# A fused clustered-attention and two-layer expert kernel: float32 probability tiles, TensorE transposes and a rewritten instruction order

## The chip, the cores and the metric

The kernel runs on one core of one Trainium2 chip. The metric is the device time of one execution in microseconds (us), lower is better.

## The reference, cut to what matters

Three parts follow one another; the output of each is the input of the next.

```
q_assign = argmax(q_n . c_n);  k_assign = argmax(k_n . c_n)      # 16 clusters, per head
scores   = where(q_assign == k_assign, q k^T / 8, -1e9)          # batch 2, 8 heads, 768 x 768, depth 64
x        = softmax(scores) v                                     # -> 1536 tokens x 512
h        = x @ w_in;  g = h * clip(h + 3, 0, 6) / 6              # 512 -> 2048
x        = g @ w_out                                             # 2048 -> 512
logits   = x @ phi                                               # 32 slots (8 experts x 4)
d        = softmax over the tokens;  slot_input = d^T x
slot_out = relu(slot_input @ w1[e]) @ w2[e]                      # 8 experts, 512 -> 1024 -> 512
out      = softmax over the slots(logits) @ slot_out             # 1536 x 512
```

w_in and w_out arrive as float64; w1 and w2 (16.8 MB each) as float32.

## The kernel before, in words

**Order.** The program is a list of some 1,130 generators ("events"), made by `ev(fn, ...)` in the body of the kernel. `ORDER`, a list of event numbers at the top of the file, says which one issues its next step; each engine works through its own instructions in exactly that order, and a semaphore wait holds up all that stands behind it on the same engine or queue. `ROOMS` says which buffer each tile takes. Event numbers, `ORDER` and `ROOMS` were written by a planner and have no loops in them.

**Attention.** There are 16 heads, 8 of batch one (0 to 7) and 8 of batch two. A head's q, k, v are loaded (`load`) and split into a float16 high part (`cast_hi`, ScalarE and VectorE) and a low part (`cast_lo`, L321 on VectorE for batch one, L323 on GpSimd for batch two); a DMA transpose from the SP queue (L361) turns them to `qk1t`. `as_mm` and `as_max` find the clusters, `as_put` (GpSimd, L417, L418) writes them as masks beside the data, and a second DMA transpose (L423) makes `qk2t`. `maxq` multiplies (L460), `maxr` takes each query's maximum on VectorE (L476, 768 columns from PSUM, 96 in all), `shift` (L483, L485) writes it back as six extra rows. `scores` (L498, L502) makes the transposed scores of one of six key tiles, `exps` (L546, L539) their exponential in float32 on ScalarE. A tile then goes one of two ways. Where `WHOLE` holds (batch one, tiles 1 and 4) the float32 tile itself is the stationary operand of six float32 matmuls (L572). Else ScalarE makes a float16 high part (L313), GpSimd a low part (`plow`, L323), and `pv` does 18 float16 matmuls (L577, L578, L585). `cnt_mm` (L432, L434, L435) gives a mean for empty clusters, added by L592 and L593; `finish` divides on VectorE.

**Weights of the first layer.** Each of 8 blocks of w_in and 8 of w_out is narrowed from float64 to float32 by integer operations on VectorE (L799, L802, L807, 1024 columns each), and multiplied on from there (`win`, `wout`, `wphi1` to `wphi3`: w_out is folded with phi to `wp2`).

**Hidden layer and routing.** The tokens are 12 tiles t of 128. Tiles 0 to 5 (batch one) are worked on beside the heads of batch two, tiles 6 to 11 after the last head. `xtrans` turns x by DMA; `hid` does 48 matmuls of 512 columns (L641); `act` applies the nonlinearity (ScalarE L658, VectorE L660, ScalarE L313, GpSimd L323), leaves `ghl` in float16 high and low, and a DMA transpose from the SP queue (L668) turns that to `gt`. `logits` (L678, L679) does 16 pairs of a 64-column and a 32-column matmul; a copy on ScalarE and an addition and a copy on VectorE follow (L682 to L686). `colmax`, `dweights` and `dispatch` (L743) keep a running softmax over the tokens, `cweights` the softmax over the slots.

**Experts and output.** `fetch` (L954, L935) streams w1 and w2 in 512 KB pieces from the SP queue into buffers ("rooms"): 4 of `ring_a`, 11 of `ring_b` that exist once attention's memory is given back (`close`), and 7 that hold the w_in blocks `w0` to `w3`, `ghl` and `gt` until those are no longer read. Pieces wait on the SP queue behind the transposes issued there. `zsum`, `slot_in`, `slot_t`, `layer1` (L1220), `turn`, `layer2` (L1257), `layer2_part` (L1277), `slots_out` and `combine` (L1197, L1205, L1207) finish; `combine_weights` turns its factors with one DMA transpose `cT` on the ScalarE queue (L1151).

Of the kernel before, what the change touches and what calls it, by code (L numbers as in the profile page):

```python
# [199 lines left out]
class Rooms:  # L200
# [6 lines left out]
    def tile(self, shape, dt, **k):  # L207
        room = self.rooms.get(k["name"])
        if room is not None:
            k["tag"] += "." + room  # L210
            k["bufs"] = 1
        return self.pool.tile(shape, dt, **k)


NRA = 4
NRB = 11


# [1132 lines left out]
```

## Time and profile before

| what | before |
|---|---|
| median of 3 runs | 523.71 us (520.7 to 527.46) |
| span of the profiled execution | 523.8 us |
| busy: TensorE (PE) / VectorE (DVE) | 445.6 us / 336.9 us |
| busy: ScalarE (ACT) / GpSimd (POOL) | 296.7 us / 277.5 us |
| moved by DMA | 100.95 MB |
| first hidden matmul / last hidden matmul | 189.6 us / 436.8 us |

The profile is of one execution, whose own time is known by its span alone; the span is within 0.1 us of the median. Busy times are shares in which an engine had an instruction running; matmuls overlap, so the distance from one start to the next says what a matmul costs in a row of them.

### The profile page before, as it was taken

The page shows a single profiled execution, that of the slowest core. Times are in us where ns is not written, and L with a number is a line of the kernel's source. Part 1 is how long each engine was busy: PE and PEld are TensorE (multiplying, and loading weights), DVE is VectorE, ACT ScalarE, POOL GpSimd, SP SyncE. Part 2 cuts the span into 40 slices and gives each one's busy share as a digit, 9 for nine tenths or more (in the row PEclk, how much of TensorE's full clock was granted, in tenths as well). Part 3 has the DMA queues.
Part 4 walks back from the last instruction along what each step waited for, and adds up shares of the span by engine and source line. Part 5 has one row for each costly group of instructions (what it writes and reads, how often), then busy time and mean ns, then how long its engine had stood idle before and what let it go on. Part 6 is the DMA issues. An engine that isn't in the chain of part 4 may idle for free. (4 is left out here: it accounts for less than half of the span.)

```text
span 523.8 us, 11918 instructions
## 1 busy us (share of the span) xinstructions
PE 445.6 (85%) x4892; PEld 268.0 (51%) x4892; DVE 336.9 (64%) x561; ACT 296.7 (57%) x491; POOL 277.5 (53%) x255
## 2 busy tenths in 40 slices
PE   0379898799889888899899999999999995698674
PEld 0225675476666656475665656664444442432152
DVE  4799999969999879997766664545343545401122
ACT  5166677668689788697847578763334445100021
POOL 3212769557799985978757768764235432000000
PEclk9999897769899999999999999999999998688796
DMA  8984564665474699445938632648999999999977
GB/s 215 282 208 87 162 168 124 162 121 147 128 194 143 182 235 228 128 124 120 167 136 146 133 112 48 177 99 159 291 245 258 240 276 265 343 271 369 367 215 230
DMA packets 155638, 100.95 MB, mean 193 GB/s; under 512 B 118208, under 2 KB 141248, under 8 KB 155584
## 3 DMA queue, kind: packets, MB, share of 16 engines
q1 hardware_dynamic: 148896, 93.97, 70.0%
q10 hardware_dynamic: 6688, 6.23, 3.8%
q8 instruction: 38, 0.62, 0.5%
q14 instruction: 16, 0.13, 0.1%
HBM read 64.06 MB, written 7.34 MB: 136 GB/s over the span
## 5 line engine op out<-in xcount | busy, mean ns | idle before, releaser
L323 POOL TENSOR_TENSOR pp<-p,pp 128x768 f16<-128x768 f32 x80 | 145.7, 1828 | 43.8 <-ACT pp L313 28.9
L641 PE MATMUL h<-wq,xt 128*128 128x512 f16 x576 | 134.4, 379 | 0.8 <-DVE r L660 0.5
L476 DVE TENSOR_REDUCE m<-sm 128x1 f32<-128x768 f32 x96 | 89.5, 952 | 27.1 <-PE sm L460 26.6
L546 ACT ACTIVATE p<-st 128x768 f32<-128x768 f32 x80 | 64.6, 810 | 47.8 <-PE st L502 27.8
L641 PEld LDWEIGHTS <-xt 128*128 128x128 f16 x576 | 53.4, 98 | 62.2 <-issue 6.3
L323 POOL TENSOR_TENSOR ghl<-r,ghl 128x1024 f16<-128x1024 f32 (+1 forms) x25 | 51.2, 2050 | 54.9 <-ACT ghl L313 54.8
L313 ACT ACTIVATE pp<-p 128x768 f16<-128x768 f32 x80 | 66.7, 840 | 5.7 <-PE acc L585 3.4
L498 PE MATMUL st<-qk1t 128*128 128x384 f16 x192 | 51.5, 352 | 9.4 <-DVE m L476 7.5
L460 PE MATMUL sm<-qk2t 80*128 80x384 f16 x192 | 51.3, 365 | 4.8 <-DVE m L476 1.8
L502 PE MATMUL st<-qk2t 102*128 102x384 f16 x192 | 51.5, 352 | 0.0
L660 DVE SCALAR_TENSOR_TENSOR r<-r,h 128x1024 f32<-128x1024 f32 (+1 forms) x26 | 29.4, 1137 | 33.3 <-ACT r L658 33.2
L577 PE MATMUL acc<-v,pp 128*128 128x65 f16 x480 | 42.5, 197 | 5.3 <-DVE oh L410 2.6
L578 PE MATMUL acc<-v,pp 128*128 128x64 f16 x480 | 42.3, 199 | 0.0
L577 PEld LDWEIGHTS <-pp 128*128 128x128 f16 x480 | 36.7, 102 | 7.1 <-DVE xa L605 2.2
L578 PEld LDWEIGHTS <-pp 128*128 128x128 f16 x480 | 34.7, 100 | 7.9 <-issue 5.1
L658 ACT ACTIVATE r<-h,b_relu 128x1024 f32<-128x1024 f32 (+1 forms) x26 | 27.0, 1048 | 19.1 <-POOL ghl L323 10.8
L313 ACT ACTIVATE ghl<-r 128x1024 f16<-128x1024 f32 (+1 forms) x26 | 25.6, 990 | 18.8 <-PE z L743 9.7
L417 POOL TENSOR_SCALAR qk<-oh 128x96 f16<-128x96 f16 x16 | 9.4, 585 | 43.3 <-DVE oh L410 43.2
L391 PE MATMUL as<-ct,qk1t 128*128 128x16 f16 x384 | 12.1, 170 | 21.3 <-DMA ct<-cin 12.5
L585 PE MATMUL acc<-v,pp 128*128 128x65 f16 x480 | 28.6, 197 | 1.1 <-POOL pp L323 1.1
L502 PEld LDWEIGHTS <-qk2t 102*128 102x128 f16 x192 | 20.2, 105 | 15.5 <-issue 4.6
L460 PEld LDWEIGHTS <-qk2t 80*128 80x128 f16 x192 | 17.7, 106 | 19.3 <-issue 11.8
(181 smaller groups left out, 814.2 us busy)
## 6 DMA issues: line engine op xcount, KB each, us to landing
wk<-in_moe_w_dram SPq DMA_DIRECT2D x60, 512.0 KB, 7.2
wi<-in_moe_w_in_dram SPq DMA_DIRECT2D x16, 512.0 KB, 5.2
wod<-in_moe_w_out_dram SPq DMA_DIRECT2D x16, 512.0 KB, 4.8
wos<-wo ACTq DMA_DIRECT2D x8, 512.0 KB, 3.6
wk<-wos SPq DMA_DIRECT2D x8, 512.0 KB, 4.4
qf<-in_q_dram SPq DMA_DIRECT2D x16, 192.0 KB, 3.3
kf<-in_k_dram SPq DMA_DIRECT2D x16, 192.0 KB, 4.2
vf<-in_v_dram SPq DMA_DIRECT2D x16, 192.0 KB, 2.9
```

The source lines that it names most:

```text
L313: nc.scalar.activation(out, in_, AF.Copy, scale=scale)
L323: (nc.vector if e == "v" else nc.gpsimd).tensor_tensor(out=out, in0=in_, in1=hi, op=ALU.subtract)
L460: nc.tensor.matmul(s[:, j, 0:384], d["qk2t"][0:80, n], d["qk2t"][0:80, NT + 3 * j : NT + 3 * j + 3], start=True, stop=True,)
L476: nc.vector.tensor_reduce(out=d["m"][:, n : n + 1], in_=s[:, :, 0:384], op=ALU.max, axis=AX.XY)
L498: nc.tensor.matmul(s[:, j, 0:384], d["qk1t"][:, NT + t], d["qk1t"][:, 3 * j : 3 * j + 3], start=True, stop=False)
L502: nc.tensor.matmul(s[:, j, 0:384], d["qk2t"][0 : 96 + NT, NT + t], d["qk2t"][0 : 96 + NT, 3 * j : 3 * j + 3], start=False, stop=True,)
L546: nc.scalar.activation(p32, s[:, :, 0:384], AF.Exp, scale=sc_exp)
L577: nc.tensor.matmul(o, hi, v1[:, t, 0:65], start=(t == 0 and n == 0), stop=False)
L578: nc.tensor.matmul(o[:, 0:64], hi, v1[:, t, 65:129], start=False, stop=False)
L585: nc.tensor.matmul(o, pl[:, j, r * P : (r + 1) * P], v1[:, t, 0:65], start=False, stop=False)
L641: nc.tensor.matmul(s[:, fb % 2], xt[:, lhs], wq[fb][:, hl, kk], start=(n == 0), stop=(n == 11))
L660: nc.vector.scalar_tensor_tensor(out=g, in0=r, scalar=6.0 * SG, in1=sf, op0=ALU.min, op1=ALU.mult)
```

## The change

Part by part:

1. **Whole tiles.** `WHOLE` now names four of the six key tiles (0, 1, 2, 4) of each head of batch one: 32 float32 tiles in place of 16, and 64 split ones in place of 80.
2. **Casts.** q and k of a head share one tile, and are scaled, split and copied in one instruction each: the scaling and the high part on ScalarE, the low part on GpSimd, for both batches (head 0 keeps VectorE). The low part of v goes to GpSimd for batch one. `as_put` moves from GpSimd to ScalarE.
3. **Full-width array forms.** `cnt_mm` takes 80 stationary columns instead of 16, `shift` 102 instead of 6, and the mean of empty clusters 128 rows instead of 32.
4. **Turned by TensorE.** For token tiles 6 to 11 (`TURNED`) `act` does 32 float16 transposes on TensorE into PSUM and four copies (two on ScalarE, two on VectorE) in place of its DMA transposes; `cT` is made by 12 such transposes.
5. **Shorter routing.** `logits` does three 32-column matmuls where it did one of 64 and one of 32, all summed in PSUM, so the addition goes; `cweights` becomes one pass over all tiles in `combine_weights`; sums of one column move to ScalarE.
6. **New order.** `ORDER` and `ROOMS` are new. Counted ahead of the first hidden matmul: VectorE's `maxr` 60 before, 53 after; cluster steps 11 and 9 heads; w_out blocks narrowed 3 and 6; and on TensorE `scores` 54 and 48 tiles, `maxq` 60 and 54, split `pv` tiles 35 and 16, whole ones 16 and 32, `wphi1` 2 and 6, `wphi2` and `wphi3` 0 and 3. All of `hid` for tiles 0 to 5 now comes before the last head's end.

The diff, cut to its core (`ORDER` and `ROOMS` left out):

```diff
+WHOLE = ("0124", "0124", "0124", "0124", "0124", "0124", "0124", "0124", "", "", "", "", "", "", "", "")
+TURNED = {6, 7, 8, 9, 10, 11}
...
     def cast_hi(i):
...
+        hi, lo = halves(d["qk1"])
+        x = d["qk"].rearrange("p a n d -> p n a d")
+        if i:
+            high("a", d["qk"], d["qk"], SQ)
+            yield
+            high("a", hi, x)
...
     def cast_lo(i):
...
-        low("p", t[:, 0, :, 64:128], d["q"], t[:, 0, :, 0:64], d["sq"])
-        yield
-        low("p", t[:, 1, :, 0:64], d["k"], t[:, 1, :, 64:128], d["sk"])
...
+        if i:
+            low("p", lo, x, hi)
...
     def as_put(i):
...
-        nc.gpsimd.tensor_scalar(out=z[:, 0, :, 64:80], in0=oh[:, 0:NT], scalar1=MASK, scalar2=0.0, op0=ALU.mult, op1=ALU.add)
...
+        nc.scalar.activation(z[:, :, 0, 64:80], oh[:, 0], AF.Copy, scale=MASK)
+        nc.scalar.activation(z[:, :, 1, 64:80], oh[:, 1], AF.Copy, scale=MASK, bias=-MASK)
...
     def cnt_mm(i):
...
-            nc.tensor.matmul(pm[64:80, 400:401], oh[:, NT + n], ones, start=(n == 0), stop=(n == NT - 1))
+            k5 = oh.rearrange("p a n c -> p (a n) c")[:, NT + n - 4 : NT + n + 1].rearrange("p n c -> p (n c)")
+            nc.tensor.matmul(pm[0:80, 400:401], k5, ones, start=(n == 0), stop=(n == NT - 1))
         for n in range(NT):
-            nc.tensor.matmul(pm[64:80, 0:65], wmean, v1[:, n, 0:65], start=(n == 0), stop=False)
+            nc.tensor.matmul(pm[0:80, 0:65], wmean, v1[:, n, 0:65], start=(n == 0), stop=False)
...
     def shift(i):
...
-        nc.tensor.matmul(pm, d["m"], nident, start=True, stop=True)
+        nc.tensor.matmul(pm, mxs[i % 2], nident, start=True, stop=True)
...
-        if WHOLE(i, t):
+        if str(t) in WHOLE[i]:
...
-    def WHOLE(i, t):
-
-        return i < H and t in (1, 4)
...
-                e = d["qk2t"][64:96, n]
-                nc.tensor.matmul(o, e, mv[64:96, 0:65], start=False, stop=False)
+                e = d["qk2t"][:, n, 0]
+                nc.tensor.matmul(o, e, mv[:, 0:65], start=False, stop=False)
...
-        nc.sync.dma_start_transpose(
-            out=d["gt"][:, f0:f1].rearrange("p a b q -> p (a b) q"), in_=g2.rearrange("p a t f -> p (a t f)")
-        )
+        if t not in TURNED:
+            nc.sync.dma_start_transpose(
+                out=d["gt"][:, f0:f1].rearrange("p a b q -> p (a b) q"), in_=g2.rearrange("p a t f -> p (a t f)")
+            )
+            return
+        tp = pss(f"gp_{t}_{f0}").rearrange("p a b -> p (a b)").bitcast(F16)[:, 0 : (f1 - f0) * 1024]
+        tp = tp.rearrange("p (f b q) -> p f b q", b=8, q=P)
+        for hl in range(2):
+            for f in range(f1 - f0):
+                for c in range(4):
+                    nc.tensor.transpose(tp[:, f, 4 * hl + c], g2[:, f, hl, c * P : (c + 1) * P], ident16)
+            yield
+        for f in range(f1 - f0):
+            if (f0 + f) % 2:
+                nc.vector.tensor_copy(d["gt"][:, f0 + f], tp[:, f])
+            else:
+                nc.scalar.copy(d["gt"][:, f0 + f], tp[:, f])
+            yield
 
     def logits(t):
...
-            nc.tensor.matmul(pl_[:, 0 : 2 * NS], gt[:, fb, c], wp2[:, f], start=(f == 0), stop=False)
-            nc.tensor.matmul(pl_[:, 0:NS], gt[:, fb, 4 + c], wp2[:, f, 0:NS], start=False, stop=(f == NF - 1))
-        yield
-        la = sm.tile([P, NS], F32, tag="la", name=f"la_{t}", bufs=2)
-        nc.scalar.copy(la, pl_[:, 0:NS])
-        yield
-        nc.vector.tensor_tensor(out=l_all[:, t], in0=la, in1=pl_[:, NS : 2 * NS], op=ALU.add)
...
+            for n, (x, w) in enumerate(((c, 0), (c, 1), (4 + c, 0))):
+                nc.tensor.matmul(
+                    pl_[:, 0:NS],
+                    gt[:, fb, x],
+                    wp2[:, f, w * NS : (w + 1) * NS],
+                    start=(f == 0 and n == 0),
+                    stop=(f == NF - 1 and n == 2),
+                )
+        yield
+        l4 = d["l4"] = sm.tile([P, 4, NS], F32, tag="l4", name=f"l4_{t}", bufs=1)
+        nc.scalar.copy(l4, pl_[:, 0:NS].unsqueeze(1).to_broadcast([P, 4, NS]))
+        yield
+        nc.scalar.copy(l_all[:, t], pl_[:, 0:NS])
...
     def combine_weights():
...
+        nc.vector.tensor_reduce(out=cx, in_=cw, op=ALU.max, axis=AX.X)
...
-        sl["cT"] = rings["cw"].tile([P, NTOK, P], F16, name="cT")
-        nc.scalar.dma_start_transpose(out=sl["cT"], in_=c16.rearrange("p t a s -> p (t a s)"))
+        yield
+        tp = pss("cTp").rearrange("p a b -> p (a b)").bitcast(F16)[:, 0 : NTOK * P].rearrange("p (t q) -> p t q", q=P)
+        for t in range(NTOK):
+            nc.tensor.transpose(tp[:, t], c16[:, t].rearrange("p a s -> p (a s)"), ident16)
+        yield
+        cT = sl["cT"] = rings["cw"].tile([P, NTOK, P], F16, name="cT")
+        nc.vector.tensor_copy(cT[:, 0:NT], tp[:, 0:NT])
+        nc.scalar.copy(cT[:, NT:], tp[:, NT:])
```

## Rows read from the trace of the kernel before

**Rows 1.** Busy time by stage (us; instructions), granted PE clock, DMA share, GB/s.

```profile
0.00:189.60 189.60, 147.03 (x1734) 103.56 (x1735) 164.56 (x251) 128.49 (x197) 122.22 (x129) 0.93 0.65 168
189.60:437.00 247.40, 239.54 (x2547) 137.17 (x2544) 151.30 (x253) 155.00 (x250) 153.50 (x125) 1.00 0.75 174
437.00:523.80 86.80, 58.99 (x623) 27.28 (x619) 21.02 (x58) 13.19 (x46) 1.80 (x3) 0.80 0.93 299
```

**Rows 2.** VectorE's groups by line: count, then busy us, mean ns, idle before.

```profile
L476 DVE TENSOR_REDUCE m<-sm 128x1 f32<-128x768 f32 x96 | 89.5, 952 | 27.1 <-PE sm L460 26.6
L807 DVE SCALAR_TENSOR_TENSOR wo<-wod,nw_o 128x1024 uint32<-128x1024 uint32 x8 | 14.8, 1847 | 0.1
L802 DVE SCALAR_TENSOR_TENSOR nw_o<-wod,nw_o 128x1024 uint32<-128x1024 uint32 x8 | 13.8, 1726 | 0.2
...
L799 DVE TENSOR_SCALAR nw_o<-nw_o 128x1024 uint32<-128x1024 uint32 x8 | 12.0, 1503 | 1.0 <-ACT nw_o L797 0.9
L321 DVE SCALAR_TENSOR_TENSOR v<-vf,v 128x384 f16<-128x384 f32 x8 | 9.2, 1153 | 0.0
...
L315 DVE TENSOR_SCALAR qk<-qf 128x384 f16<-128x384 f32 x8 | 5.8, 726 | 5.3 <-DMA qf<-in_q_dram 3.0 <-DMA qk1t<-qk 2.1
...
L321 DVE SCALAR_TENSOR_TENSOR qk<-qf,qk 128x384 f16<-128x384 f32 x8 | 4.9, 617 | 0.1
L321 DVE SCALAR_TENSOR_TENSOR qk<-kf,qk 128x384 f16<-128x384 f32 x8 | 4.8, 606 | 0.6 <-ACT qk L313 0.6
```

**Rows 3.** TensorE in order of time (start us, duration us): split tile, whole tile.

```profile
68.23 0.19 PE L577 MATMUL acc<-v,pp 128*128 128x65 f16 x1
...
68.61 0.48 PE L498 MATMUL st<-qk1t 128*128 128x384 f16 x2
...
91.75 1.45 PE L572 MATMUL acc<-v,pp 128*128 128x65 f32 x12
93.04 0.49 PE L460 MATMUL sm<-qk2t 80*128 80x384 f16 x2
```

**Rows 4.** TensorE in order of time: narrow forms between full ones, then float32 transposes.

```profile
226.28 0.34 PE L585 MATMUL acc<-v,pp 128*128 128x65 f16 x6
226.56 0.20 PE L592 MATMUL acc<-mv,qk2t 32*128 32x65 f16 x1
...
226.91 0.19 PE L593 MATMUL acc<-mv,qk2t 32*128 32x64 f16 x1
227.03 1.09 PE L867 MATMUL tp<-ident,wo 128*128 128x128 f32 x8
227.96 0.49 PE L498 MATMUL st<-qk1t 128*128 128x384 f16 x2
```

**Rows 5.** TensorE's weight loads of 32 and of 96 float32 columns, by line.

```profile
L1220 PEld LDWEIGHTS e<-wk,sts 128*32 128x32 f32 x128 | 5.0, 126 | 12.3 <-issue 11.8 <-DVE sts L1126 0.5
...
L1172 PEld LDWEIGHTS so<-o2s,sel 128*96 128x96 f32 x12 | 1.4, 162 | 1.7 <-DVE o2s L1288 1.3 <-issue 0.4
```

**Rows 6.** TensorE in order of time: the 32 matmuls of logits, 24 of the hidden layer.

```profile
359.30 0.19 PE L678 MATMUL lg<-wp,gt 128*128 128x64 f16 x1
...
360.17 2.75 PE L641 MATMUL h<-wq,xt 128*128 128x512 f16 x12
...
362.87 5.34 PE L641 MATMUL h<-wq,xt 128*128 128x512 f16 x24
368.14 0.24 PE L729 MATMUL pe<-ident,et 32*128 32x32 f32 x1
```

**Rows 7.** The tail: busy time by stretch, columns as in rows 1.

```profile
450.00:465.00 15.00, 12.32 (x121) 6.35 (x125) 5.05 (x17) 1.72 (x12) 0.00 (x0) 0.74 1.02 376
465.00:475.00 10.00, 9.98 (x96) 2.79 (x88) 0.00 (x0) 0.00 (x0) 0.00 (x0) 1.00 0.87 200
```

**Rows 8.** Two pieces of the chain that ended last (start us, us, what).

```profile
442.46 4.81 DMA gt<-ghl
...
457.27 11.59 DMA cT<-c
```

More of the change, by code (lines that the diff above doesn't have):

```diff
@@ L283, in clustered_attention_ffn_softmoe @@
     NZ, NV = 3, 3
-    qk2 = [ap.tile([P, 2, NT, P], F16, name=f"qk2_{i}", bufs=1) for i in range(NZ)]
+    qk2 = [ap.tile([P, NT, 2, P], F16, name=f"qk2_{i}", bufs=1) for i in range(NZ)]
     v1s = [ap.tile([P, NT, 129], F16, name=f"v1_{i}", bufs=1) for i in range(NV)]
     v32s = [ap.tile([P, NT, 65], F32, name=f"v32_{i}", bufs=1) for i in range(3)]
+    mxs = [ap.tile([P, 96 + NT], F32, name=f"mxs_{i}", bufs=1) for i in range(2)]
     mvs = [ap.tile([P, 129], F16, name=f"mv_{i}", bufs=1) for i in range(3)]
@@ L302, in consts @@
         for t in mvs:
-            nc.gpsimd.memset(t[64:96], 0.0)
+            nc.gpsimd.memset(t, 0.0)
+        for t in mxs:
+            nc.gpsimd.memset(t, 0.0)
         nc.gpsimd.memset(b_relu, 3.0 * SG)
@@ L330, in load @@
         b, h = divmod(i, H)
-        for nm, src in (("q", q), ("k", k)) if part == 0 else (("v", v),):
-            t = ap.tile([P, NT, D], F32, tag="ld" + nm, name=f"{nm}f_{i}", bufs=1 if nm == "v" else 2)
-            nc.sync.dma_start(out=t, in_=src[b, h].rearrange("(p n) d -> p n d", n=NT))
-            st[i][nm] = t
+        if part == 0:
+            t = st[i]["qk"] = ap.tile([P, 2, NT, D], F32, tag="ld", name=f"qk_{i}", bufs=2)
+            for n, src in enumerate((q, k)):
+                nc.sync.dma_start(out=t[:, n], in_=src[b, h].rearrange("(p n) d -> p n d", n=NT))
+                yield
+        else:
+            t = st[i]["v"] = ap.tile([P, NT, D], F32, tag="ldv", name=f"v_{i}", bufs=1)
+            nc.sync.dma_start(out=t, in_=v[b, h].rearrange("(p n) d -> p n d", n=NT))
@@ L335, in load, with halves @@
             yield
+    def halves(t):
+        x = t.rearrange("p n a (h d) -> p n (a h) d", h=2)
+        return x[:, :, 0:4:3], x[:, :, 1:3]
     def cast_hi(i):
         d = st[i]
-        t = ap.tile([P, 2, NT, P], F16, tag="qk1", name=f"qk1_{i}", bufs=1)
-        d["qk1"] = t
-        b = i // H
-        for nm in "qk":
-            d["s" + nm] = SQ
-            if b:
-                high("a", d[nm], d[nm], SQ)
-                d["s" + nm] = 1.0
+        d["qk1"] = ap.tile([P, NT, 2, P], F16, tag="qk1", name=f"qk1_{i}", bufs=1)
+        hi, lo = halves(d["qk1"])
[4 more added lines that the diff above has]
+            high("a", hi, x)
+        else:
+            for a, e in enumerate("va"):
+                high(e, hi[:, :, a], x[:, :, a], SQ)
@@ L347, in cast_hi @@
                 yield
-        high("a" if b else "v", t[:, 0, :, 0:64], d["q"], d["sq"])
-        yield
-        high("a", t[:, 1, :, 64:128], d["k"], d["sk"])
     def cast_lo(i):
         d = st[i]
-        t = d["qk1"]
-        z = qk2[i % NZ]
-        low("p", t[:, 0, :, 64:128], d["q"], t[:, 0, :, 0:64], d["sq"])
+        hi, lo = halves(d["qk1"])
+        x = d["qk"].rearrange("p a n d -> p n a d")
+        if i:
+            low("p", lo, x, hi)
+        else:
+            for a in range(2):
+                low("v", lo[:, :, a], x[:, :, a], hi[:, :, a], SQ)
+                yield
@@ L375, in castv_hi @@
         yield
-        high("a", v1s[i % NV][:, :, 0:64], d["v"], sc)
-        d["sv"] = sc
+        high("a", v1s[i % NV][:, :, 0:64], f[:, :, 0:64])
     def castv_lo(i):
         v1 = v1s[i % NV]
-        low("p", v1[:, :, 65:129], st[i]["v"], v1[:, :, 0:64], st[i]["sv"])
+        low("p", v1[:, :, 65:129], st[i]["v32"][:, :, 0:64], v1[:, :, 0:64])
         yield
@@ L408, in as_max @@
         nc.vector.tensor_reduce(out=mx2, in_=sc, op=ALU.max, axis=AX.X)
-        oh = ap.tile([P, 12, C], F16, tag="oh", name=f"oh_{i}")
-        nc.vector.tensor_tensor(out=oh, in0=sc, in1=mx2.unsqueeze(2).to_broadcast([P, 12, C]), op=ALU.is_equal)
+        oh = ap.tile([P, 2, NT, C], F16, tag="oh", name=f"oh_{i}")
+        nc.vector.tensor_tensor(
+            out=oh.rearrange("p a n c -> p n a c"),
+            in0=sc.rearrange("p (n a) c -> p n a c", a=2),
+            in1=mx2.rearrange("p (n a) -> p n a", a=2).unsqueeze(3).to_broadcast([P, NT, 2, C]),
+            op=ALU.is_equal,
+        )
         d["oh"] = oh
@@ L455, in maxq @@
         d = st[i]
-        if "m" not in d:
-            d["m"] = sm.tile([P, NT], F32, tag="m", name=f"m_{i}", bufs=2)
         s = pss(f"sm_{i}_{n}")
@@ L975, in clustered_attention_ffn_softmoe @@
     for i in range(NH):
+        if i == H:
+            for t in range(NT):
+                ev(xtrans, t)
         if i >= 2:
@@ L1040, in clustered_attention_ffn_softmoe @@
             ev(hid, t, fb, 0, 1)
-        if t < NTOK - 1:
-            ev(act, t, 0, 2)
-            ev(act, t, 2, 4)
-        else:
-            for fb in range(4):
+            if t == NTOK - 1:
                 ev(act, t, fb, fb + 1, fb == 3)
+            elif fb % 2:
+                ev(act, t, fb - 1, fb + 1)
         ev(logits, t)
@@ L1130, in combine_weights @@
         cw = l_all
+        cx = sm.tile([P, 12], F32, tag="mx", name="cx", bufs=2)
+        nc.vector.tensor_reduce(out=cx, in_=cw, op=ALU.max, axis=AX.X)
+        yield
+        nc.vector.tensor_tensor(out=cw, in0=cw, in1=cx.unsqueeze(2).to_broadcast([P, NTOK, NS]), op=ALU.subtract)
+        yield
+        nc.scalar.activation(cw, cw, AF.Exp, scale=LSC)
+        yield
+        nc.vector.tensor_reduce(out=csum, in_=cw, op=ALU.add, axis=AX.X)
+        yield
         nc.vector.tensor_scalar(out=csum, in0=csum, scalar1=1e-9, scalar2=1.0 / SC, op0=ALU.add, op1=ALU.mult)
```

98 lines of the change are left out of this document (42 added, 56 removed), and 324 rows, old and new, of tables (ORDER, ROOMS).

## The prediction, made before the changed kernel ran

> **What bounds the kernel now.** I read the busy times by stage first and cut the span at two events: the first hidden-layer matmul (189.6 us) and the last (436.8 us). That gives three stages with three different bounds [rows 1]. Stage A, up to the first hidden matmul, is VectorE's: it is busy 164.6 of 189.6 us (87%), TensorE only 147.0 (78%), with a granted clock of 0.93, so that some 27 us of it lie at 1.2 GHz instead of 2.4. The reader is to see that no other engine is near: ScalarE has 128, GpSimd 122. Stage B, to the last hidden matmul, is TensorE's: 239.5 of 247.4 us (97%) at a clock of 1.00, with VectorE at 61%. What is added to TensorE here is added to the time, nearly one for one. Stage C, the tail, belongs to no engine (TensorE 59 of 87 us); DMA is busy 93% and moves 299 GB/s. The grouped lines then gave the durations, the order of time what a matmul costs in a row of them, and the chain of waits what the tail hangs on: a turned `gt` of 4.81 us, then `cT` of 11.59 us, then weights [rows 8]. The profiled span (523.8 us) is within 0.1 us of the median, so the sum against the span is the forecast of the median.
>
> **Stage A: VectorE.** Its casts of q and k go for seven of eight heads: 7/8 of 5.8 (L315) and of 4.9 + 4.8 (L321), 13.6 us; the low part of v goes whole, 9.2 us [rows 2]. That is 22.8 us less. The new order also moves work across the cut. Seven of the query maxima come later (7 x 0.93 = 6.5 us), and with them some 13 shorter steps of two heads, which I put at half a maximum each, 6.2 us, an estimate. Three more blocks of w_out come earlier, (14.8 + 13.8 + 12.0) / 8 = 5.1 us each, 15.2 us, and 1.3 us of folding. Net: -22.8 - 12.7 + 16.5 = -19.0, so VectorE has 145.6 us, and at the same 87% the stage would last 168 us.
>
> TensorE nearly catches up. A split tile is 18 matmuls, 12 of them in 68.61 - 68.23 = 0.38 us, so 0.57; a whole tile takes 93.04 - 91.75 = 1.29 us, since its float32 passes load 128 columns each at 107 ns [rows 3]. Sixteen more whole tiles cost 16 x 0.72 = 11.5 us here. (They take 16 x 18 matmuls' operands off ScalarE and GpSimd, which don't bound this stage; that is worth waits only.) What moves in (4 `wphi1` at 0.93 [rows 4], three folds, about 9 us) and out (6 `scores`, 6 `maxq`, 3 split tiles and small steps, about 9 us) cancels. TensorE would be busy some 160 of 168 us, were its clock as before; it fits only if fewer of its 27 slow microseconds remain. I add 2 us for that: stage A 170 us, against 189.6. Its bounds: 162 (VectorE's integer steps lengthened by less GpSimd traffic, and 90% busy) and 188 (TensorE's 160 us at 85%).
>
> The casts' price on the other side: GpSimd takes q, k and v of batch one and gives up 16 `plow` and `as_put`, and ScalarE takes the scaling and gives up 16 high parts; both stay under 80% of 170 us, so I cost them at nothing; were the cover gone, at most the 5 to 10 us that each gains in wait would show, inside the bounds.
>
> **Narrow and wide forms.** A switch from full to narrow and back leaves a gap: six L585 at 0.031 from 226.28 would end at 226.47, L592 starts at 226.56; from L593 at 226.91 to the next full form 227.03 it is 0.09 again [rows 4]. Three narrow groups per head make six gaps, 0.54 us saved. Against this, 18 matmuls of `cnt_mm` load 80 columns instead of 16. The trace has no such float16 load. From below it costs nothing (31 ns each, as now), from above 107 ns, the 128 float32 columns. Loads of 32 and 96 float32 columns take 126 and 162 ns [rows 5], so columns do count; at 107/128 ns per column 80 columns are 67 ns, which I take as the nearest: 18 x 0.036 = 0.65 us, and 0.1 for `shift`. Net +0.2 us a head, between -0.54 and +0.9; over 16 heads +3, between -9 and +14. For stage A 1.6, already inside its margin; for B 1.4.
>
> The Trainium skill speaks against the wide form (TensorE: Matmul & The Clock Gate, section on weight-path perf modes): fast weight loading is on only for exactly 128 columns that are not float32, and otherwise a load takes its columns over 1.2 GHz. No row here shows an 80-column load; by that rule it is 67 ns and the sum stands, by the spacing of the 16-column rows alone the total would be 10 us lower.
>
> **Stage B: TensorE.** Transposes: ten of the twelve groups of 16 (token tiles 6 to 10) stand ahead of the last hidden matmul or next to it, 160 in all. The trace has no float16 transpose. From below a small full-width matmul costs (360.17 - 359.30)/32 = 27 ns [rows 6], from above a float32 transpose (227.96 - 227.03)/8 = 116 ns [rows 4]. It streams 128 columns; 24 matmuls of 512 take 5.27 us, 0.43 ns a column [rows 6], so I take 56 ns: 9.0 us (4.3 to 18.6). Logits: 16 more matmuls of 27 ns for 11 tiles, 4.8 us. Wide forms 1.4. Work moved across the cut, about +0.4. Together +15.6: stage B 263 us. The 24 copies of 1024 columns from PSUM (VectorE and ScalarE, about 1.2 us each by a 768-column maximum's 0.95) lie beside TensorE, as do the routing's steps: VectorE is at 61% here and loses the additions and copies.
>
> The Trainium skill gives about 275 ns for such a transpose inside a kernel (same page, Part 4: PE-mode transpose). The float32 transposes have that duration too, but a spacing of 116 ns, so the trace says that they overlap; by 275 ns each the total would be 35 us more.
>
> **Stage C: the tail.** The last `gt` turned by DMA (4.81 us on the chain [rows 8]) becomes 8 transposes a block, 0.5 us, and a copy of 1.2 us: 3.1 less, and the shorter routing takes 0.5 more. `cT` by DMA holds up the weight stream: 376 GB/s before it, 200 in the ten microseconds in which it lands [rows 7]; the missing 1.8 MB are 4.7 us at 376 GB/s. The DMA time that the last four `gt` took from weights between 440 and 450 us I put at 2 us, an estimate. Together 10: stage C 77 us, between 87 (weights come as late as before, since 7 of the 22 rooms open only when the last hidden blocks are read) and 71 (both transfers vanish whole, 16.4). After that the chain ends on the last weight pieces and `layer2_part`, as now.
>
> **Sum:** 170 + 263 + 77 = 510 us.
>
> **Rivals.**
> 1. *Everything fits* (TensorE stays at 2.4 GHz in stage A and wide loads cost nothing): 162 + 260 + 75 = 497. For it: 27 slow microseconds and 42 idle ones in A to win from. Against: two engines at over 90% that feed each other.
> 2. *TensorE takes over stage A*: its 160 us at 85% are 188 us, so VectorE's relief buys nothing and float32 is paid: 188 + 263 + 77 = 528. For it: it never passed 78% there.
> 3. *The tail keeps its length*, since the same weights are outstanding when the last rooms open: 170 + 263 + 87 = 520. For it: 376 GB/s is already near what DMA shows anywhere.
> 4. *PSUM rooms* (the slower end). The transposes write into the same three two-bank PSUM rooms as hidden blocks and scores; each of the 10 groups of 16 must wait for a room and give it back only after its copies, and TensorE stands behind that wait with all hidden work. At 3 us a group, two copies and the steps between, it is 30 us in B: 540. It makes the kernel slower than before from 1.4 us a group on. Against: three rooms, a hidden pair needs 5.3 us to fill, and a copy is 1.2 us.
> 5. *Transposes cost their duration*, 1.09 - 7 x 0.116 = 0.28 us each without overlap: 160 x 0.22 more, 545. That is the duration of the float32 transposes [rows 4], taken as if nothing overlapped; their spacing is against it. The Trainium skill's Part 4 (TensorE: Matmul & The Clock Gate) speaks for it.
>
> That the change doesn't do what it says I see no way to: the counts are in the code.
>
> **How the numbers follow.** Forecast (503 to 517) 0.46, rival 1 0.17, rival 2 0.15, rival 3 0.10, rival 4 0.09, rival 5 0.03. Over 2% faster (about what a measurement of this kernel can tell from no change) is below 513.2 us: rival 1 whole, three quarters of the forecast, a little of rival 3: 0.52. Slower by over 2%, above 534.2: rivals 4 and 5 and the edge of rival 2: 0.12. The rest, 0.36, is within. The range 496 to 532 leaves out half of rival 1 below and rivals 4 and 5 with some of 2 above, about 0.2.
>
> **What would show it.** Right: the first hidden matmul near 170 us with VectorE still about 87% busy before it, the last near 433, no `gt` transfers and no dip in GB/s after it, whole tiles at 1.29 us, transposes 56 ns apart, `cnt_mm` matmuls near 67 ns apart. Wrong: TensorE as the busiest engine of stage A with a clock below 0.93 (rival 2); gaps ahead of transposes that end on copies (rival 4); a tail of 87 us (rival 3). If stage B grows by more than 20 us, my price for what TensorE took on is wrong.

## The result and the profile after the change

| | before | after |
|---|---|---|
| median of four runs each on one chip (us) | 525.59 | 505.17 |
| span of the profiled execution (us) | 523.8 | 503.8 |
| ratio of the times | | 0.965 (0.957 to 0.973) |
| stage A, to the first hidden matmul | 189.6 | 163.8 (forecast 170) |
| stage B, to the last hidden matmul | 247.4 | 264.4 (forecast 263) |
| stage C, the tail | 86.8 | 75.6 (forecast 77) |

The hidden matmul is L650 now. Its first one starts at 163.8 us, its last ends at 428.2. The first view is that of [rows 1]: busy time by stage for TensorE matmul, weight load, VectorE, ScalarE and GpSimd, then the granted clock, the DMA share and GB/s.

```profile
0.00:163.80 163.80, 139.36 (x1583) 112.27 (x1584) 134.50 (x215) 122.68 (x182) 83.73 (x99) 0.98 0.78 201
163.80:428.20 264.40, 254.02 (x2922) 152.77 (x2922) 126.19 (x216) 173.79 (x280) 152.80 (x105) 0.99 0.56 141
428.20:503.80 75.60, 55.51 (x697) 28.07 (x693) 21.89 (x48) 14.48 (x35) 3.21 (x14) 0.93 0.95 318
```

In stage A VectorE lost 30 us and TensorE 8, at a clock of 0.98 in place of 0.93; over the whole stage they stand at 82 and 85% now. These averages hide something: from 40 us on, TensorE is busy 97% of the time, where it was 88% in the kernel before (the kernel before, then the changed one):

```profile
40.00:189.60 149.60, 130.96 (x1607) 95.91 (x1607) 136.40 (x196) 111.50 (x169) 112.74 (x78) 0.91 0.58 151
40.00:163.80 123.80, 120.52 (x1413) 99.63 (x1411) 106.62 (x163) 97.83 (x147) 68.78 (x45) 0.97 0.73 193
```

So there TensorE, and no longer VectorE, is the busiest engine. GpSimd fell from 122 to 84 us although it took the casts: it also gave up the subtractions of 16 tiles and `as_put`, and other work moved behind the cut. Stage B is TensorE's as before (96%), longer by 17 us. The DMA share of stage B fell from 0.75 to 0.56.

The shorter steps of VectorE, which answer to the L802, L807 and L799 lines of [rows 2], for the first 163.8 us (count, then busy us and mean ns of one, then idle before):

```profile
L822 DVE SCALAR_TENSOR_TENSOR wi<-wi,nw_i 128x1024 uint32<-128x1024 uint32 x8 | 11.2, 1394 | 0.4
L817 DVE SCALAR_TENSOR_TENSOR nw_i<-wi,nw_i 128x1024 uint32<-128x1024 uint32 x8 | 9.8, 1225 | 0.2
...
L817 DVE SCALAR_TENSOR_TENSOR nw_o<-wod,nw_o 128x1024 uint32<-128x1024 uint32 x6 | 7.4, 1226 | 0.2
L822 DVE SCALAR_TENSOR_TENSOR wo<-wod,nw_o 128x1024 uint32<-128x1024 uint32 x6 | 7.3, 1224 | 0.3
```

No shape changed, yet L817 takes 1226 ns on `nw_o` where L802 took 1726 over the whole execution [rows 2] and 1521 for the three blocks in its first stage; L822 takes 1224 where L807 took 1847 and 1536.

The new operations, in TensorE's order of time (start us, duration us): one group of 16 transposes between hidden matmuls; then the first and the last of the twelve `cnt_mm` matmuls on 80 columns of one head, and the full form behind them.

```profile
375.60 1.07 PE L687 MATMUL gp<-ident,ghl 128*128 128x128 f16 x16
376.51 2.75 PE L650 MATMUL h<-wq,xt 128*128 128x512 f16 x12
```

```profile
215.20 0.20 PE L449 MATMUL cm<-v,wmean 128*80 128x65 f16 x1
...
215.62 0.20 PE L450 MATMUL cm<-v,wmean 128*80 128x64 f16 x1
215.66 0.20 PE L586 MATMUL acc<-v,pp 128*128 128x65 f16 x1
```

Transposes stand (376.51 - 375.60)/16 = 57 ns apart, as forecast. The 80-column forms stand (215.62 - 215.20)/11 = 38 ns apart, not 67, and the full form follows them without a gap.

Last, SyncE's own waits from 350 to 440 us (engine and line, what it waited for: us, times, longest), and two stretches by the columns of [rows 1]:

```profile
SPq L969 <- PE h L650: 48.0, 3, 43.1
```

```profile
363.00:378.00 15.00, 14.41 (x152) 8.32 (x149) 4.17 (x8) 8.50 (x14) 4.26 (x2) 1.00 1.03 412
378.00:416.00 38.00, 36.27 (x370) 20.61 (x369) 12.90 (x21) 17.11 (x32) 12.52 (x18) 1.00 0.12 48
```

With no `gt` in the queue the weights run at 412 GB/s until every open room is full; then SyncE waits 43 us in one piece for a room that the hidden matmuls still read, and DMA is nearly idle. In the kernel before, DMA was busy without a pause there, at far fewer bytes:

```profile
365.00:437.00 72.00, 69.93 (x517) 32.64 (x516) 31.54 (x62) 28.90 (x54) 27.89 (x38) 1.00 1.07 258
```

Even so, by the last hidden matmul both kernels had issued the same number of weight pieces, 26 of 68 (count; ns: shortest, median, longest; first and last start in us; the kernel before, then the changed one to 428.0 us):

```profile
L954 SPq DMA_DIRECT2D wk<-in_moe_w_dram x26: 429/434/1122, 365.0 to 435.4; - x26
L969 SPq DMA_DIRECT2D wk<-in_moe_w_dram x26: 327/366/1982, 355.5 to 424.7; - x26
```

So the total came out 5 us below the forecast, and the three stages at 6 less, 1 more and 1 less. Whether for the forecast's reasons, the experiments had to show: each undoes, doubles or extends one part in the changed kernel, or puts one part, once three, into the kernel before. The profiled executions of `e2_narrow_forms`, `e6_before_casts` and `e7_before_wide` lie 1.6 to 1.8% above the fastest of their kernels, so their stages are read to a few us only.

### The profile page after: what moved, and what is told of

Read it like the earlier page. It is cut to its first block, busy times and chain, and to the rows that moved or that the text cites. A ratio compares the mean times of both kernels' runs of the same rounds, so it can differ in the third digit from the quotient of the medians.

```text
span 503.8 us, 12322 instructions
## 1 busy us (share of the span) xinstructions
PE 448.9 (89%) x5192; PEld 293.1 (58%) x5192; DVE 282.6 (56%) x477; ACT 311.0 (62%) x495; POOL 239.7 (48%) x218
## 2 busy tenths in 40 slices
DMA packets 129046, 94.28 MB, mean 187 GB/s; under 512 B 91616, under 2 KB 114656, under 8 KB 128992
## 4 chain that ended last, share of the span: by engine, by line
PE 65%; DMA 9%; DVE 8%; ACT 7%; POOL 4%; issue 4%; SPq 3%; POOLq 0%; ACTq 0%; DVEq 0%
PE h L650 19%; PE st L511 6%; PE st L515 5%; PE acc L581 5%; PE sm L473 5%; PE e L1248 3%; PE lg L703 2%; DMA wod<-in_moe_w_out_dram 2%; DVE mxs L489 2%; DMA qk2t<-qk 2%; PE acc L594 2%; PE acc L586 2%; PE acc L587 2%; POOL pp L327 2%; DMA wk<-in_moe_w_dram 1%
## 5 line engine op out<-in xcount | busy, mean ns | idle before, releaser
L327 POOL TENSOR_TENSOR pp<-p,pp 128x768 f16<-128x768 f32 x64 | 108.4, 1700 | 64.3 <-ACT pp L317 36.6
L650 PE MATMUL h<-wq,xt 128*128 128x512 f16 x576 | 134.9, 384 | 2.3 <-DMA xt<-xhl 2.1
L489 DVE TENSOR_REDUCE mxs<-sm 128x1 f32<-128x768 f32 x96 | 88.7, 951 | 32.9 <-PE sm L473 32.0
L650 PEld LDWEIGHTS <-xt 128*128 128x128 f16 x576 | 54.9, 99 | 64.3 <-issue 3.9
L317 ACT ACTIVATE pp<-p 128x768 f16<-128x768 f32 x64 | 53.3, 840 | 1.1
L581 PEld LDWEIGHTS acc<-v,pp 128*128 128x128 f32 x384 | 47.6, 196 | 2.4 <-DVE xa L614 0.6
L581 PE MATMUL acc<-v,pp 128*128 128x65 f32 x384 | 48.0, 277 | 0.2 <-DVE xa L614 0.2
L327 POOL TENSOR_TENSOR qk<-qk,qk 128x768 f16<-128x768 f32 x15 | 25.2, 1683 | 27.0 <-ACT qk L317 19.4
L552 ACT ACTIVATE pp<-st 128x768 f32<-128x768 f32 x32 | 25.7, 810 | 12.9 <-PE st L515 12.8
L586 PE MATMUL acc<-v,pp 128*128 128x65 f16 x384 | 32.3, 193 | 0.8 <-ACT pp L317 0.7
L586 PEld LDWEIGHTS <-pp 128*128 128x128 f16 x384 | 27.7, 99 | 3.8 <-ACT pp L317 1.1
L317 ACT ACTIVATE qk<-qk 128x768 f32<-128x768 f32 (+2 forms) x31 | 25.5, 827 | 6.2 <-DMA qk<-in_k_dram 3.1
L587 PEld LDWEIGHTS <-pp 128*128 128x128 f16 x384 | 26.2, 97 | 2.4 <-issue 0.5
```

The lines of the kernel that those rows point to most:

```text
L317: nc.scalar.activation(out, in_, AF.Copy, scale=scale)
L327: (nc.vector if e == "v" else nc.gpsimd).tensor_tensor(out=out, in0=in_, in1=hi, op=ALU.subtract)
L489: nc.vector.tensor_reduce(out=mxs[i % 2][:, 96 + n : 97 + n], in_=s[:, :, 0:384], op=ALU.max, axis=AX.XY)
L581: nc.tensor.matmul(o, p32[:, j, r * P : (r + 1) * P], d["v32"][:, t], start=(t == 0 and n == 0), stop=False)
L586: nc.tensor.matmul(o, hi, v1[:, t, 0:65], start=(t == 0 and n == 0), stop=False)
L587: nc.tensor.matmul(o[:, 0:64], hi, v1[:, t, 65:129], start=False, stop=False)
```

## Experiments

Each ratio is to the kernel before, on the same chip, with its 95% interval. To put the changed kernel's 0.965 beside them, 0.01 is 5.2 us. "First hidden" and "last hidden" are the cuts between the stages. The first stages of the changed kernel and of the three runs that leave it alone (the two DMA turns and the doubled transposes) were 163.8, 168.2, 165.3 and 161.8 us at clocks of 0.98, 0.95, 0.96 and 0.99: that is how far one profiled execution can be trusted. In the old order the last run below, which only turns `cT` on TensorE, leaves the first stage alone too, and there it took 185.5 us in place of 189.6:

```profile
0.00:185.50 185.50, 145.62 (x1735) 102.51 (x1736) 164.15 (x251) 128.53 (x196) 122.36 (x130) 0.94 0.65 169
```

So a first stage that is some 4 us shorter or longer in one profile shows nothing by itself.

**The casts, taken back in the new order.**

```diff
-            low("p", lo, x, hi)
+            low("v" if i < H else "p", lo, x, hi)
```

and the same for `v` in `castv_lo`.

> The changed kernel with the low parts of q, k and v of batch one (15 subtractions) on VectorE again; the order stays. They add 7 x 1.1 us (768 columns at twice the 0.56 us of 384) and 8 x 0.6 to 1.15 us, 12.5 to 17 us, to VectorE's 134.5 us of the first stage (163.8 us). Theory T (from about 40 us on TensorE bounds that stage: 120.5 of 123.8 us busy, and VectorE has slack): the first hidden matmul moves by 0 to 5 us, total 505 to 510. Theory V (VectorE still bounds it, as the prediction has it, at 82 to 87% busy): the first hidden matmul at 178 to 184 us, total 519 to 526, and TensorE's clock in the stage falls back towards 0.93.

Ratio 0.9996 (0.994 to 1.005): the whole gain was gone. First hidden at 180.4 us:

```profile
0.00:180.40 180.40, 145.33 (x1582) 115.32 (x1583) 147.19 (x230) 123.20 (x181) 65.85 (x84) 0.95 0.70 183
```

VectorE got 147.19 - 134.50 = 12.7 us more and the stage grew by 16.6. It is still 9 us shorter than before the change; that the total is as long as before comes of the other stages, 265.2 and 77.5 us here, which together are 8.5 us longer than before. TensorE's waits show the way: those of `sm` for VectorE's maxima (`mxs`) are longer here than in the changed kernel (us, times, longest; here, then there):

```profile
PE sm L473 <- DVE mxs L489: 8.4, 4, 6.6
PE sm L473 <- DVE mxs L489: 1.5, 2, 0.9
```

Only q and k taken back:

> The changed kernel with only the low parts of q and k of seven heads on VectorE (7.8 us of the 12.7 that the run with q, k and v moved); those of v stay on GpSimd. Theory V (VectorE's work is on the path, so its price is in proportion: 16.6 us of stage for 12.7): first hidden matmul at 172 to 176 us, total 512 to 517. Theory Q (what cost there was the v part, which stands ahead of cnt_mm and the attention sums, and not the sum of VectorE's work): first hidden matmul at 164 to 168 us, total 503 to 508.

Ratio 0.979 (0.974 to 0.984), first hidden at 172.6 us:

```profile
0.00:172.60 172.60, 140.64 (x1583) 112.55 (x1584) 140.68 (x222) 123.12 (x182) 73.38 (x92) 0.98 0.72 190
```

That is 8.8 us of stage for 6.2 of VectorE, at the same clock. Both runs are theory V: in the new order VectorE is on the path, and a microsecond on it costs about one or somewhat more; the spread of untouched first stages (161.8 to 168.2) does not allow a closer figure.

**The same casts, alone in the old order.**

```diff
-        high("a" if b else "v", t[:, 0, :, 0:64], d["q"], d["sq"])
+        if i and not b:
+            d["sq"] = d["sk"] = 1.0
+            high("a", d["q"], d["q"], SQ)
+        high("a" if i else "v", t[:, 0, :, 0:64], d["q"], d["sq"])
```

and likewise k and v; the low parts then go to GpSimd.

> The kernel before with only the casts of batch one moved: the scaling of q, k, v on ScalarE, their low parts on GpSimd; old order, two whole tiles, narrow forms. Theory V (VectorE bounds the first stage): 22.8 us of 164.6 leave it, at 87% busy the stage shortens by 12 to 24 us, total 500 to 512. Theory G (GpSimd, 122 us busy in that stage, takes 22 subtractions of some 0.9 us, slows VectorE's integer steps, and the old order waits for them): total 515 to 526.

Ratio 0.999 (0.993 to 1.004): nothing.

```profile
0.00:184.00 184.00, 141.86 (x1733) 100.60 (x1734) 146.58 (x222) 138.15 (x218) 142.41 (x151) 0.95 0.67 173
```

VectorE lost 18 us of busy time; the stage is 5.6 us shorter than in the kernel before and 1.5 shorter than the untouched one above. GpSimd rose from 122 to 142 us, or 77%. The total is theory G's, but not its mechanism: the 33 integer steps of the stage took 48.9 us, where they took 48.4. What grew is VectorE's wait for the products whose maxima it takes (the kernel before, then here; us, times, longest):

```profile
DVE m L476 <- PE sm L460: 5.4, 4, 2.6
DVE m L483 <- PE sm L467: 13.8, 11, 4.5
```

The step of the forecast that takes VectorE's relief over "at the same 87%" does not hold in this order.

**Four whole tiles, alone in the old order; six in the new one.**

```diff
-        return i < H and t in (1, 4)
+        return i < H and t in (0, 1, 4, 5)
```

> The kernel before with four whole key tiles (0, 1, 4, 5) a head in batch one in place of two; nothing else changed. Theory P (a whole tile costs TensorE 0.72 us more, and VectorE bounds the stage): TensorE +11.5 us in the first stage; between 0 (hidden in its waits) and 11.5 us of it show, total 524 to 535. Theory G (the 16 subtractions of about 1.7 us that leave GpSimd let VectorE's integer steps, 1.5 to 1.7 us each, run shorter, and VectorE bounds the stage): total 514 to 522.

Ratio 1.004 (0.997 to 1.011).

```profile
0.00:184.50 184.50, 149.87 (x1638) 110.87 (x1639) 156.67 (x251) 116.81 (x181) 90.29 (x113) 0.98 0.69 172
```

The stage came out 5 us shorter than in the kernel before, but only 1 us shorter than the untouched one above, so no gain of it is shown; nor did 16 dearer tiles on TensorE make it longer. VectorE ran the same 251 instructions in 156.7 us in place of 164.6 (164.2 in the untouched one). The line L802 on `nw_i`, first before the change, then here (ns: shortest, median, longest):

```profile
L802 DVE SCALAR_TENSOR_TENSOR nw_i<-wi,nw_i x8: 1215/1506/2611, 13.6 to 138.6; 128x1024 uint32<-128x1024 uint32 x8
```

```profile
L802 DVE SCALAR_TENSOR_TENSOR nw_i<-wi,nw_i x8: 1215/1224/1305, 14.0 to 135.6; 128x1024 uint32<-128x1024 uint32 x8
```

So theory G is right on its mechanism: what leaves GpSimd (122 to 90 us) shortens VectorE's steps. But the total did not follow, and theory P has the total. In the other direction, the changed kernel with all six tiles whole (`WHOLE` "012345" for "0124"; in head 7 the last tile reads `v` values that head 10 has put in the same room, so the output differs, while the number and shapes of the instructions are those of six whole tiles):

> The changed kernel with all six key tiles of batch one whole in place of four, order unchanged: TensorE gets 16 x 0.72 = 11.5 us more in the first stage, ScalarE, GpSimd and through it VectorE get less. Theory T (TensorE bounds that stage from about 40 us on, where it was busy 120.5 of 123.8 us): first hidden matmul at 172 to 177 us, total 513 to 518. Theory V (VectorE sets the pace and TensorE's additions fit between): first hidden matmul at 162 to 167 us, total 503 to 508.

Ratio 0.979 (0.975 to 0.983), 7.4 us worse than the changed kernel.

```profile
0.00:167.40 167.40, 146.21 (x1487) 121.50 (x1488) 132.60 (x215) 112.29 (x165) 54.56 (x83) 1.00 0.76 197
```

The first stage is 3.6 us longer than in the changed kernel, and 5.6 longer than in the doubled transposes' run, whose clock (0.99) is nearest; TensorE has 9.1 us more than there. By itself that length is within the spread of untouched first stages, and 5.3 of the 8.9 us by which the profile is longer lie in stages that the edit leaves alone. The stretch from 40 us on says more:

```profile
40.00:167.40 127.40, 127.40 (x1314) 108.98 (x1312) 103.41 (x162) 86.72 (x127) 39.67 (x29) 1.00 0.70 186
```

TensorE is busy without a pause, at a clock of 1.00. Against the changed kernel it has 6.9 us more of busy time, and 3.3 us of waits are gone, which leaves the 3.6 us. Of the rest of the 11.5 us priced, the higher clock paid about (1.00 - 0.97) x 123.8 = 3.7 us, an estimate from the two granted clocks. So with six tiles TensorE bounds the stage from 40 us on, and with four it nearly does. The number fell between the theories since waits and clock had something left to give.

**The wide forms.** Narrow again in the changed kernel, then wide alone in the kernel before:

```diff
-            nc.tensor.matmul(pm[0:80, 0:65], wmean, v1[:, n, 0:65], start=(n == 0), stop=False)
+            nc.tensor.matmul(pm[64:80, 0:65], wmean[:, 64:80], v1[:, n, 0:65], start=(n == 0), stop=False)
```

and so on for the other forms.

> The changed kernel with the three narrow forms again (cnt_mm from 16 columns, mv from 32 rows, shift from 6 columns). Theory W (the wide forms keep the granted clock up): the first stage's clock falls from 0.98 to about 0.93 and it grows by 7 us or more, total 511 to 516. Theory S (the clock follows how little TensorE waits, the forms only cost what their spacing shows): the clock stays at 0.97 to 0.98; the gaps cost 0.54 us a head more and the loads 0.75 less, so the total is 502 to 508. By the measured spacing of the 80-column loads against the 31 ns of the narrow ones the total could fall by up to 5 us.

Ratio 0.960 (0.947 to 0.974), first stage 166.0 us at 0.97: no difference from the changed kernel that can be told.

> The kernel before with only the wide forms (cnt_mm from 80 columns, mv from 128 rows, shift from 102 columns). Theory W (full forms raise the granted clock): the first stage's clock rises from 0.93 to 0.97 or more, and the total falls by 5 to 10 us, 514 to 519. Theory S (the clock follows TensorE's waits for VectorE): clock 0.92 to 0.95, total 522 to 528.

Ratio 0.992 (0.986 to 0.998), first stage at a clock of 0.95. Both are theory S: the forms do not carry the clock. At 38 ns against the 32 of the narrow form (L434 to L435 of the kernel before, eleven steps from 297.83 to 298.18 us) they cost 18 x 6 ns = 0.1 us a head and save the gaps, 0.5. For 16 heads that is some 6 us, an estimate from these spacings; the 4 us of the ratio 0.992 fit it, but the run with narrow forms in the changed kernel, whose interval is 14 us wide, cannot confirm it.

**Casts, forms and whole tiles together in the old order.**

> The kernel before with casts moved, wide forms and four whole tiles together, in the old order. Theory O (these edits carry the first stage's gain of 26 us, and the order little): first hidden matmul at 163 to 172 us, total 498 to 507. Theory N (the new order carries at least half of the gain): first hidden matmul at 175 to 185 us, total 510 to 520.

Ratio 1.005 (1.000 to 1.010).

```profile
0.00:185.40 185.40, 150.50 (x1639) 117.47 (x1640) 140.64 (x222) 127.19 (x202) 112.50 (x138) 0.96 0.70 172
```

Theory N, even beyond its range: VectorE is relieved by 24 us and TensorE is at 81%, yet first hidden comes at 185.4 us, as in the untouched stage above. With VectorE at 76%, TensorE at 81%, ScalarE at 69% and GpSimd at 61% no engine is full. The relief went into VectorE's wait for the same products, 5.4 us in the kernel before:

```profile
DVE mxs L486 <- PE sm L470: 19.5, 16, 4.3
```

The engines work off lists whose order is written out, and in the old list the products for the maxima did not come early enough when VectorE was ready earlier. That the new order is what makes the difference is an inference: this run leaves out the merging of q and k and the move of `as_put`, and no run has the new order with the old parts.

From the first piece of `w1` to the end, DMA is full in the old order, in the kernel before and here:

```profile
365.00:523.80 158.80, 128.92 (x1134) 59.92 (x1132) 52.56 (x120) 42.09 (x100) 29.69 (x40) 0.89 0.99 280
```

```profile
363.70:523.50 159.80, 127.82 (x1128) 59.78 (x1126) 51.93 (x119) 41.98 (x100) 28.60 (x39) 0.88 1.03 278
```

The piece leaves 1.3 us earlier, and the stretch from there on is as long as in the kernel before. In the runs with four tiles, with casts and with wide forms it starts 1.4 to 3.8 us earlier and takes 163 to 168 us. Whether a full DMA swallows an earlier start is not shown by this: in the untouched stage above the piece leaves 3.9 us earlier too, and the rest, with `cT` on TensorE, takes 152 us. Most of the changed kernel's 26 us were missing before this stretch began, in the first stage.

**Batch two turned by DMA again** (`TURNED = set()` in the changed kernel).

> The changed kernel with batch two's activations turned by DMA again: no transposes on TensorE, no copies from PSUM. Theory P (the priced sum: transposes cost TensorE 57 ns each in the hidden stage, and the last gt and the weights it delays cost the tail 3 to 5 us): hidden stage 9 to 11 us shorter, tail 3 to 6 longer, total 498 to 503. Theory D (with the weights ahead of it in the queue, a turned block comes late, and logits and dispatch behind it stall TensorE): transposes are worth it, total 506 to 515.

Ratio 1.028 (1.019 to 1.038): 32 us lost, far outside both theories. It is D's sign, but D's mechanism is small: in the hidden stage TensorE waited 4.8 us for turned blocks, about half of the 9 us that the missing transposes should have saved. Stage B is 264.4 us long, just as with the transposes on TensorE, and the tail 107.5. SyncE's waits from 350 to 440 us, then two stretches by the columns of [rows 1]:

```profile
SPq L678 <- POOL ghl L327: 29.2, 8, 7.7
SPq L678 <- PE lg L703: 14.4, 5, 5.4
```

```profile
375.00:432.60 57.60, 53.16 (x398) 24.44 (x398) 14.60 (x23) 22.66 (x43) 19.06 (x22) 0.96 0.37 72
432.60:510.00 77.40, 54.03 (x434) 19.07 (x430) 13.45 (x31) 8.21 (x23) 3.22 (x14) 0.80 1.00 364
```

SyncE issues both the turns (L678) and the weights (L969), in the order written. Each turn waits for its low part from GpSimd and for the logits that free `gt`, and the weight pieces behind it wait too (13 turns in a row keep them back from 366 to 439 us): 72 GB/s in the 58 us before the cut, and then 77 us at the full rate after it, which is pure tail. Only 3 of the 68 pieces were issued before the cut, against 26 in the changed kernel:

```profile
L969 SPq DMA_DIRECT2D wk<-in_moe_w_dram x3: 345/423/572, 360.2 to 365.8; - x3
```

The 23 others are 12.1 MB, 33 us at 364 GB/s, and the tail is 31.9 us longer: the count of pieces accounts for the loss. This order was written for a queue without those turns, so the 32 us are the price of the turn in this order, not in the old one; in the old one, turns and all, 26 pieces had been issued by the last hidden matmul.

**The transposes twice.**

```diff
-                    nc.tensor.transpose(tp[:, f, 4 * hl + c], ...)
+                    for _r in range(2):
+                        nc.tensor.transpose(tp[:, f, 4 * hl + c], ...)
```

> The changed kernel with each of the 192 transposes of batch two's activations issued twice. Theory P (each takes its spacing, 57 ns, off TensorE's path): 160 in the hidden stage 9.1 us, 32 in the tail 1.8 us, total 513 to 518. Theory H (they lie in the some 10 us in which TensorE waits in that stage): total 504 to 509. Theory L (each costs about the 0.22 us of its duration): total 535 or more.

Ratio 0.975 (0.971 to 0.980), 5.4 us worse than the changed kernel.

```profile
161.80:432.90 271.10, 261.91 (x3078) 161.47 (x3078) 127.15 (x218) 174.40 (x281) 152.75 (x105) 0.99 0.56 140
```

Stage B is 6.7 us longer for 160 more transposes: 42 ns each, three quarters of the spacing. In the changed kernel and the five other runs of its order that turn each block once on TensorE, stage B was 263.7 to 266.1 us, so this is 31 to 46 ns. TensorE is busy 7.9 us more; about 1 us lay in its waits. The total fell between P and H, nearer to P in the stage; theory L is out.

**The combine weights turned by DMA.** In the changed kernel the old transpose comes back:

```diff
-        for t in range(NTOK):
-            nc.tensor.transpose(tp[:, t], c16[:, t].rearrange("p a s -> p (a s)"), ident16)
...
+        nc.scalar.dma_start_transpose(out=sl["cT"], in_=c16.rearrange("p t a s -> p (t a s)"))
```

> The changed kernel with the combine weights turned by the DMA transpose again. Theory C (the transpose holds up the weight stream as the prediction counted it, 4.7 us): the tail is 3 to 6 us longer, with a stretch near 200 GB/s, total 508 to 512. Theory N (the stream catches up, or the tail's end hangs on the rooms and on layer 2 whatever cT does): total 504 to 507.

Ratio 0.981 (0.976 to 0.987), 8.6 us worse than the changed kernel; the tail:

```profile
429.60:512.50 82.90, 57.73 (x686) 30.10 (x682) 21.42 (x47) 13.70 (x34) 3.23 (x14) 0.87 0.94 294
```

7.3 us longer, more than theory C's 6, at 294 GB/s in place of 318. The same edit forwards, alone in the kernel before:

> The kernel before with only the combine weights turned by TensorE (12 transposes and two copies) in place of the DMA transpose; old order. Theory C (the DMA transpose holds up the weight stream wherever it stands): the tail is 4 to 8 us shorter than 87, total 516 to 522. Theory O (the tail's gain needs the new order too): tail 85 to 88 us, total 523 to 527.

Ratio 0.988 (0.983 to 0.993).

```profile
432.70:513.50 80.80, 55.25 (x634) 26.66 (x630) 21.57 (x59) 13.97 (x47) 1.76 (x3) 0.84 0.98 316
```

The tail is 6.0 us shorter than 86.8, which is the shortest of the five tails measured in the old order with `cT` by DMA (up to 95.8). Both are theory C: this is the one part that pays by itself in either order, since the end of both kernels hangs on the weight stream. It is 1.2% of the 3.5%.

## Why the prediction was right, point by point

**Stage A (forecast 170, measured 163.8).** The sign and most of the size were right, and VectorE's casts were the right cause, but the sum reached it by steps of which three were off.
- "VectorE has 145.6 us": it had 134.5. The integer steps were taken at the old durations: 48.4 us of them in the old stage plus 15.2 moved in, 63.6. They measured 46.2 (all six groups of the three lines, 42 instructions). The forecast had their shortening only as a bound (162 us). The run with four whole tiles shows that GpSimd's relief can do it: the same 33 steps fell from 48.4 to 40.8 us. For the changed kernel this is likely but not shown by itself. Less GpSimd work alone does not set their length: with the casts back on VectorE, GpSimd had 18 us less and the steps took 45.2.
- "TensorE would be busy some 160 of 168 us, were its clock as before": 139.4. The clock did not stay: 0.98. That is worth about 10 us, an estimate: some 27 us at 1.2 GHz became some 7, each half lost. The other 10 us stay open. The wide forms are not why the clock rose; the clock was also 0.98 with four whole tiles in the old order, and 0.95 with the casts back on VectorE, where TensorE waits more.
- "At the same 87%": the share was 82%, and in the old order it fell to 76% with nearly the same relief. The share is no constant of the stage; it goes with the order. This is the step that failed as reasoning: a part's worth was computed as if it were independent of the order, and the runs show that casts, tiles and forms together are worth 0 in the old order, while the low parts of the casts alone are worth all 3.5% in the new one. The step came out right since the forecast was for both at once, and by luck: 134.5 us at 87% would be 155 us, and 145.6 us at 82% would be 178. The two errors have opposite signs and nearly cancel. Nor is it VectorE that sets the pace now, as the forecast had it: from 40 us on TensorE is the fuller engine.

**Forms.** The 67 ns for an 80-column load was too dear: 38 ns. By the column rule of the Trainium skill (TensorE: Matmul & The Clock Gate, sections on LDWEIGHTS and on weight-path perf modes) the estimate is 67 ns, 80 columns over 1.2 GHz; the trace agrees neither in the spacing, 38 ns, nor in the load's own record, 128 ns for 80 columns (93 for 16), and the measurement decides. With 38 ns the forecast's sum gives -0.3 us a head in place of +0.2, which is -5 us for 16 heads in place of +3: by these spacings, which no run resolves better than the 0.992 above, the term had the wrong sign, and its error of 8 us is larger than that of the total.

**Whole tiles.** 12 matmuls of a whole tile take 1.29 us as before. The price of 0.72 us a tile showed on TensorE (six whole: 9.1 us more for 11.5 priced), and less of it on the stage, as far as one profile can tell. Of rival 2 the time fell with the clock: no stage of 188 us. Its mechanism came half true, since TensorE is busy 97% from 40 us on.

**Stage B (263, measured 264.4).** Transposes at 57 ns for the 56 forecast; doubled, they cost 42. Rival 5 is out. The Trainium skill's Part 4 (same page) gives about 275 ns for such a transpose inside a kernel: the trace disagrees, with 219 ns for the duration of one, 57 ns of spacing and 42 ns for each of a second set. Rival 4 fell too: the copies take 1.00 us on ScalarE and 0.69 on VectorE (1.2 forecast), and TensorE waited 0.2 us in all for one of them.

**Stage C (77, measured 75.6).** The term for `cT` was 4.7 and measured 6.0 and 7.3 us. The forecast's terms add up to 9.3 us (3.1 - 0.5 + 4.7 + 2), which it rounded to 10; the tail lost 11.2. Rival 3 fell. What the forecast put at 5 us for the last `gt` cannot be separated by a run: taken back, they cost 32 us, because of the queue. In the kernel before, SyncE issued no weight piece from 435.9 to 443.8 us, and spent 5.9 us of that on four turns; this fits the term but does not show what it was worth.

**What the forecast did not see** is that DMA is full over the last 159 us of the kernel before: the row at 365 to 437 us has TensorE at 97% and DMA at 1.07 at once. Taking the 14 turns of `gt` and that of `cT` off DMA (100.95 MB to 94.28 by the pages' queue lines, 155,638 packets to 129,046) emptied it there. It is not shown that this moved a bound. Both kernels had issued 26 weight pieces by the last hidden matmul, so up to there the turns had cost the old stream no piece against the changed kernel. The turning of `gt` by TensorE in the old order was not tried, since its list has no place for those steps; what it is worth there stays open. Which moved steps make the new first stage short stays open as well.

No version beat the changed kernel: the one with narrow forms (0.960, 0.947 to 0.974) cannot be told from it.

## What to carry to other kernels

Where the order of every queue is written out, price a part together with the order it will run in. Relief of a busy engine can turn into waits on the same engine (5.4 us became 19.5 here), and a part taken out of a list made for it can cost far more than it brought. An average over a stage can hide its bound: TensorE at 85% was 97% from 40 us on. A transfer that waits for a computed operand holds everything behind it in its queue. Count the bytes that stand behind it at the end of the stage, not its own duration: 23 pieces late were 32 us, while a DMA that was full while 26 pieces went out had lost none.

## What the runs showed of the hardware that was not expected

VectorE and GpSimd delay each other within single instructions. Three rows of the kernel before, in order of time:

```profile
121.09 0.91 POOL L323 TENSOR_TENSOR qk<-qf,qk 128x384 f16<-128x384 f32 x1
121.19 1.90 DVE L802 SCALAR_TENSOR_TENSOR nw_i<-wi,nw_i 128x1024 uint32<-128x1024 uint32 x1
121.97 1.90 POOL L323 TENSOR_TENSOR qk<-kf,qk 128x384 f16<-128x384 f32 x1
```

The step whose shortest duration is 1.215 us takes 1.90 when it starts behind a subtraction of GpSimd. The next subtraction, of the same shape as the 0.91 us one, takes 1.90 too and ends 0.78 us after VectorE's step. The Trainium skill (SBUF — State Buffer, section on who interferes with whom) says that the two engines share a pair of ports and that one holds it for a whole instruction; the trace agrees, as far as these three rows go. With 16 subtractions fewer on GpSimd, 33 such steps took 7.6 us less (48.4 to 40.8), which a price list of old durations hides.

DMA at a share of about 1 moved 412 GB/s with weights alone (363 to 378 us, after) and 258 with `gt` turns among them (365 to 437 us, before). Whether a turn costs anything by that depends on whether bytes are missing later: here both kernels had issued 26 pieces by the last hidden matmul.
